# One pool of four PSUM banks for layer 1 of a fused attention and two feed-forward layers, with the attention of later batches merged into fewer TensorE visits and placed anew

## Chip, core and metric

One core of a Trainium2 chip runs the whole program. The metric is the device time in microseconds (us) of one execution. TensorE, VectorE, ScalarE and GpSimd appear as PE, DVE, ACT and POOL; SyncE (SP) issues the DMAs.

## What is computed

Attention with 32 landmarks (a Nystrom approximation), then two feed-forward layers on its 2304 x 512 output. B, H, S, D are 4, 8, 576, 64, and m is 32:

```python
q_lm = q.reshape(B, H, m, S // m, D).mean(axis=3)
k_lm = k.reshape(B, H, m, S // m, D).mean(axis=3)
A, Bm, C = sm(q, k_lm), sm(q_lm, k_lm), sm(q_lm, k)     # sm: scaled scores, softmax
Z = Bm^T / (norm1(Bm) * norminf(Bm) + 1e-6)
for _ in range(6):
    Z = 2 * Z - Z @ Bm @ Z
x = A @ Z @ C @ v                                       # heads back into rows of 512
h = x @ w_in;  x = (h * clip(h + 3, 0, 6) / 6) @ w_out                      # layer 1
h = x @ w2_in; out = (P(h) / (Q(h) + 1e-6)) @ w2_out                        # layer 2
```

Inputs are drawn as float64 for the weights (the kernel reads their bits as 64-bit integers and makes float32 of them) and the output is float32.

## The kernel before, in words

The work runs in two stages. **Layer 1** holds the attention of the four batches and the first feed-forward layer; **layer 2** is a pipeline of its own at the end of `fused` and is not touched by the diff.

Layer 1 works on blocks of 288 tokens (two a batch, eight in all) and on 16 chunks of 128 hidden features per block, 128 chunks in all. For each chunk `l1_in` multiplies U by A: six matmuls of 128x288 in float32r into a bank `psh`. U = T x w_in is the product of the attention's small matrix T (per head, 64x32) with the first weight, so that A x U is the hidden layer. ScalarE then makes the relu `r` and VectorE the gate `g` (the clipped product), which frees the bank. `l1_split` splits g into a high and a low half, `ghl` (ScalarE and GpSimd), and `l1_out` multiplies it by the second weight: twelve matmuls into four banks `psy`, which add up over the 16 chunks of a block. `l1_out` of a chunk stands LEAD = 3 chunks behind its `l1_in`.

Between the chunks stand the attention of the next batch and the conversion of weights (`cv_bits`: one operation on ScalarE and three on VectorE per slab of 128x1024; `cv_split` and stores behind it). The attention of a batch from 1 on is a chain: landmarks; the scores of C and of the landmark matrix (`scores_c`); transposes of exp(C) (`transpose_e`); `landmark_matrix`; the first E and V of the Newton iteration (`first_e`, `first_v`); six steps `newton` for each of two groups of four heads, which hold E as a 128x128 matrix with four 32x32 blocks on the diagonal and V beside it; T (`tmat`); the softmax of A for each half of the tokens (`scores_a`, `soft_a1` to `soft_a3`); and four `u_pair`, each of which makes U of one pair of slabs out of two slabs `wis` loaded again from DRAM. `by_head` issues the matmuls for eight heads: 64 rows by 32 columns each, four heads into either of two banks.

PSUM has eight banks: four `psy`, two `psa` for the attention, two `psh` for chunks (in batch 0 also for attention).

What sets the order: every piece of work is put into a list `plan` with a place, counted in chunks (`at`), and the list is emitted sorted by place. Numbers in `PRM` give the places of the start and of the conversions; for batches 1 to 3 `chain_c`, `chain_a` and the loop over `b` give them as fixed offsets. A scheduler in the framework then moves instructions on each engine's queue, so that the queues do not follow the plan exactly. All DMAs go through SP's queue in order. Slabs of weights, U and parts of y share 31 buffers.

Of the kernel before, what the change touches and what calls it, by code (L numbers as in the profile page):

```python
# [20 lines left out]
LM = 32  # L21
# [30 lines left out]
    d2=0,
    ta=5.46,
# [7 lines left out]
def fused(ctx: ExitStack, tc: tile.TileContext, qT, kT, v, w_in, w_out, w2_in, w2_out, ca, cb, out):  # L61
# [131 lines left out]
    def psa(tag="psa"):  # L193
        return pp.tile([P, 512], F32, tag=tag, name=tag, bufs=2 if tag in ("psa", "psh") else 1)
# [37 lines left out]
    def scores_a(b, h):  # L232
        sT = att.tile([P, 18, LM], F32, tag="sT", name="sT", bufs=1)
        pss = [psa("psh" if b == 0 else "psa") for _ in range(2)]
        by_head(
            pss, slice(0, HB),
            lambda r, a: kx[b][r:r + 64, a, S:S + LM],
            lambda r, a: qx[b][r:r + 64, a, h * HB:(h + 1) * HB],
        )
        for g in range(2):  # L240
            V.transpose(sT[:, 9 * g:9 * g + 9, :].rearrange("p a m -> p (a m)"), pss[g][:, :HB])
        st[b, h, "sT"] = sT
# [27 lines left out]
    def scores_c(b):  # L270
# [3 lines left out]
        end = [psa() for _ in range(2)]  # L274
        by_head(
            end, slice(0, TN + LM),
            lambda r, a: qs[r:r + 64, a, :], lambda r, a: kx[b][r:r + 64, a, 512:S + LM],
        )
        if b == 0:
            far = end  # L280
            big = [psa("psh") for _ in range(2)]
        else:

            far = []
            for g in range(2):
                t = att.tile([P, TN + LM], F32, tag=f"ce{g}", name="ce", bufs=1)
                A.activation(t, end[g][:, 0:TN + LM], AF.Copy)
                far.append(t)
            big = [psa() for _ in range(2)]
# [15 lines left out]
        for g in range(2):  # L305
            e = att.tile([P, S], F32, tag="e", name="e", bufs=2)
# [7 lines left out]

    def landmark_matrix(b):
# [4 lines left out]
        V.tensor_tensor(sm[:, :, 2], sm[:, :, 0], sm[:, :, 1], op=ALU.add)  # L320
# [29 lines left out]
        st[b, "bd"], st[b, "rc"] = bd, rc  # L350
# [13 lines left out]
    def first_e(b, g):  # L364
        bd, rc = st[b, "bd"], st[b, "rc"][:, 1]
        ps = psa()
        t = bd[:, 1, g].rearrange("p a m -> p (a m)")
        PE.matmul(ps[:, 0:P], t, t, start=True, stop=True)
        ev = att.tile([P, P + D], F32, tag=f"ev{g}", name="ev", bufs=2)
# [3 lines left out]
    def first_v(b, g):
        eT, rc, ev = st.pop((b, g, "eT")), st[b, "rc"][:, 0], st[b, g, "ev"]
        ps = psa("psh" if b == 0 else "psa")
        for c in range(5):
            n = P if c < 4 else 64
            for h in range(4):
                PE.matmul(
                    ps[LM * h:LM * h + LM, 0:D],  # L380
                    eT[0:n, c, LM * h:LM * h + LM],
                    vx[b][0:n, c, (2 * h + g) * D:(2 * h + g + 1) * D],
                    start=(c == 0), stop=(c == 4),
                )
        A.activation(ev[:, P:P + D], ps[:, 0:D], AF.Copy, scale=rc[:, g:g + 1])

    def newton(b, g, k):
        ev = st[b, g, "ev"]
        nx = att.tile([P, P + D], F32, tag=f"ev{g}", name="ev", bufs=2)
        last = k == NITER - 1  # L390
        if b == 0:

            x = ev[:, P:P + D]
# [7 lines left out]
            PE.matmul(vs, ev[:, 0:P], x, start=True, stop=True)  # L401
            if not last:
                V.tensor_tensor(nx[:, P:P + D], vs, x, op=ALU.add)
            else:
                V.tensor_tensor(nx[:, 0:D], vs, x, op=ALU.add)
        else:
            n0 = P if last else 0
            ps = psa()
            vs, x = ps[:, P:P + D], ev[:, P:P + D]
            PE.matmul(ps[:, n0:P + D], ev[:, 0:P], ev[:, n0:P + D], start=True, stop=True)  # L410
            if not last:
                A.activation(nx[:, 0:P], ps[:, 0:P], AF.Copy)
# [428 lines left out]
```

## Time and profile before

| | us |
|---|---|
| median of 3 runs (lowest, highest) | 873.9 (870.58, 874.69) |
| the profiled execution | 875.29 |
| its span in the profile | 873.5 |
| PE busy | 834.2 (96%) |
| PE weight loads busy | 748.6 (86%) |
| DVE, ACT, POOL busy | 577.2 (66%), 474.9 (54%), 483.2 (55%) |

Busy is the time in which at least one instruction of the engine runs. Matmuls overlap in the record (a 128x288 matmul is recorded with some 300 ns but the next one starts 130 ns later), so the pace of starts tells more than the length of one. A float32 matmul stands twice in the trace and once in the order listings. The profile has the span, its shares by engine, groups of instructions by line, the waits, the chain of work that ended last, and stretches of time with the busy time of each engine.

### The profile page before, as it was taken

The page shows a single profiled execution, that of the slowest core. Times are in us where ns is not written, and L with a number is a line of the kernel's source. Part 1 is how long each engine was busy: PE and PEld are TensorE (multiplying, and loading weights), DVE is VectorE, ACT ScalarE, POOL GpSimd, SP SyncE. Part 2 cuts the span into 40 slices and gives each one's busy share as a digit, 9 for nine tenths or more (in the row PEclk, how much of TensorE's full clock was granted, in tenths as well). Part 3 has the DMA queues.
Part 4 walks back from the last instruction along what each step waited for, and adds up shares of the span by engine and source line. Part 5 has one row for each costly group of instructions (what it writes and reads, how often), then busy time and mean ns, then how long its engine had stood idle before and what let it go on. Part 6 is the DMA issues. An engine that isn't in the chain of part 4 may idle for free.

```text
span 873.5 us, 14948 instructions
## 1 busy us (share of the span) xinstructions
PE 834.2 (96%) x5766; PEld 748.6 (86%) x5766; DVE 577.2 (66%) x910; ACT 474.9 (54%) x876; POOL 483.2 (55%) x353
## 2 busy tenths in 40 slices
PE   9679989999999899998999999999999999999998
PEld 8558879788977789888999899898998998989986
DVE  6967895776576945766215876765766666666566
ACT  3434654465445634655434666565665655656564
POOL 1438364465345533577331886766676685675542
PEclk9768999999999999999999999999999999999999
DMA  9765464669148740595797010010010010000000
GB/s 354 275 226 168 147 229 167 225 201 334 38 158 287 253 163 28 189 327 197 262 324 254 1 37 8 30 37 1 37 37 1 37 36 1 37 1 1 37 1 36
DMA packets 46310, 113.16 MB, mean 130 GB/s; under 512 B 6176, under 2 KB 14368, under 8 KB 45856
## 3 DMA queue, kind: packets, MB, share of 16 engines
q1 hardware_dynamic: 46240, 112.22, 36.7%
q8 instruction: 45, 0.74, 0.3%
q14 instruction: 25, 0.20, 0.1%
HBM read 81.79 MB, written 30.41 MB: 128 GB/s over the span
## 4 chain that ended last, share of the span: by engine, by line
PE 66%; DVE 15%; DMA 6%; ACT 6%; issue 4%; POOL 2%; SPq 0%; DVEq 0%; ACTq 0%; POOLq 0%
PE po L740 20%; PE ph L687 20%; PE psy L490 14%; PE psh L467 7%; DMA raw<-in_moe_w_out 3%; DVE val L142 2%; DVE val L143 2%; PE psa L227 2%; DMA qx<-in_q 2%; DVE g L472 1%; ACT val L140 1%; PE psa L410 1%; DVE val L141 1%; DMA yr<-yd 1%; DMA yd<-y 1%
## 5 line engine op out<-in xcount | busy, mean ns | idle before, releaser
L490 PE MATMUL psy<-ghl,whi 128*128 128x288 f32 x1024 | 225.3, 304 | 6.7 <-POOL ghl L99 4.4
L99 POOL TENSOR_TENSOR ghl<-g,ghl 128x288 fp32r<-128x288 f32 x128 | 127.4, 999 | 151.8 <-ACT ghl L94 143.1
L740 PE MATMUL po<-w2s,g2hl 128*128 128x512 f32 x864 | 209.6, 396 | 1.5 <-POOL g2hl L99 1.5
L687 PE MATMUL ph<-yhl,w2s 128*128 128x384 f32 x1152 | 208.5, 336 | 0.6 <-DVE y L518 0.6
L687 PEld LDWEIGHTS ph<-yhl,w2s 128*128 128x128 f32 x1152 | 202.1, 188 | 4.5 <-DVE y L518 0.8
L740 PEld LDWEIGHTS po<-w2s,g2hl 128*128 128x128 f32 x864 | 161.3, 188 | 37.9 <-POOL g2hl L99 2.9
L490 PEld LDWEIGHTS psy<-ghl,whi 128*128 128x128 f32 x1024 | 169.7, 191 | 16.9 <-issue 7.3
L490 PE MATMUL psy<-ghl,wlo 128*128 128x288 f32 x512 | 150.4, 299 | 0.0
L467 PE MATMUL psh<-AT,us 128*128 128x288 f32 x768 | 134.7, 308 | 12.5 <-DVE g L472 11.4
L467 PEld LDWEIGHTS psh<-AT,us 128*128 128x128 f32 x768 | 112.9, 194 | 25.5 <-DVE g L472 16.3
L717 DVE SCALAR_TENSOR_TENSOR q<-q,r 128x768 f32<-128x768 f32 (+1 forms) x52 | 46.6, 896 | 114.2 <-ACT r L712 114.2
L699 POOL TENSOR_SCALAR q<-t,cb_s 128x768 f32<-128x768 f32 x44 | 56.5, 1283 | 100.9 <-ACT t L697 100.9
L99 POOL TENSOR_TENSOR g2hl<-g,g2hl 128x768 fp32r<-128x768 f32 (+1 forms) x52 | 89.7, 1726 | 32.4 <-ACT g2hl L94 32.4
L472 DVE SCALAR_TENSOR_TENSOR g<-r,psh 128x288 f32<-128x288 f32 x128 | 56.8, 448 | 73.4 <-ACT r L470 65.2
L94 ACT ACTIVATE ghl<-g 128x288 fp32r<-128x288 f32 x128 | 56.2, 442 | 83.1 <-DVE g L472 75.9
L490 PEld LDWEIGHTS psy<-ghl,wlo 128*128 128x128 f32 x512 | 97.8, 191 | 0.9 <-issue 0.9
L470 ACT ACTIVATE r<-psh,three 128x288 f32<-128x288 f32 x128 | 63.1, 498 | 56.8 <-PE psh L467 56.6
L711 ACT ACTIVATE r<-q,lnb 128x768 f32<-128x768 f32 (+1 forms) x52 | 46.2, 889 | 81.8 <-POOL q L700 76.3
L99 POOL TENSOR_TENSOR wlo<-val,whi 128x1024 fp32r<-128x1024 f32 x24 | 59.9, 2496 | 52.1 <-ACT whi L94 48.9
L700 POOL TENSOR_TENSOR q<-q,t 128x768 f32<-128x768 f32 x44 | 84.5, 1920 | 3.7
L697 ACT ACTIVATE t<-ph 128x384 f32<-128x384 f32 x96 | 46.9, 489 | 56.5 <-PE ph L687 55.9
L718 DVE SCALAR_TENSOR_TENSOR p<-p,ca_s,r 128x768 f32<-128x768 f32 (+1 forms) x52 | 64.6, 1243 | 0.0
(144 smaller groups left out, 1016.3 us busy)
## 6 DMA issues: line engine op xcount, KB each, us to landing
raw<-in_moe_w_in SPq DMA_DIRECT2D x32, 512.0 KB, 5.9
raw<-in_moe_w_out SPq DMA_DIRECT2D x32, 512.0 KB, 5.3
wis<-wid SPq DMA_DIRECT2D x24, 512.0 KB, 7.4
w2s<-w2di SPq DMA_DIRECT2D x16, 512.0 KB, 6.0
w2s<-w2do SPq DMA_DIRECT2D x16, 512.0 KB, 5.9
yd<-y SPq DMA_DIRECT2D x32, 144.0 KB, 2.9
out<-o SPq DMA_DIRECT2D x18, 256.0 KB, 2.0
vx<-in_v SPq DMA_DIRECT2D x4, 1024.0 KB, 8.5
```

Source lines behind the costliest of these rows:

```text
L94: A.activation(dst_hi, src, AF.Copy)
L99: lo_eng.tensor_tensor(dst_lo, src, dst_hi.bitcast(F32), op=ALU.subtract)
L467: PE.matmul(ps[:, :HB], u[:, wp, f0:f0 + P], at[:, xp, g, :], start=(k == 0), stop=(k == 5))
L470: A.activation(r, ps[:, :HB], AF.Relu, bias=three)
L472: V.scalar_tensor_tensor(gg, in0=r, scalar=6.0, in1=ps[:, :HB], op0=ALU.min, op1=ALU.mult)
L490: PE.matmul(ps[e][:, :HB], w1[c // 2][wp][:, o + e * P:o + (e + 1) * P], t[:, xp, :], start=(c == c0 and i == 0), stop=(c == c1 and i == 2),)
L687: PE.matmul(ps[i][:, :T2], w2i[u][wp][:, d * 256 + i * P:d * 256 + (i + 1) * P], yh[:, xp, d, :], start=(k == 0), stop=(k == 11),)
L697: A.activation(t[:, i], h, AF.Abs)
L699: eng.tensor_scalar(q[:, cs], t[:, cs], cb_s[:, 1:2], cb_s[:, 0:1], op0=ALU.mult, op1=ALU.add)
L700: eng.tensor_tensor(q[:, cs], q[:, cs], t[:, cs], op=ALU.mult)
L718: V.scalar_tensor_tensor(p, in0=p, scalar=ca_s[:, 0:1], in1=r, op0=ALU.add, op1=ALU.mult)
L740: PE.matmul(ops[j][m], t[:, xp, i, m * P:(m + 1) * P], w2o[u][wp][:, i * DM:(i + 1) * DM], start=(c == 0 and k == 0), stop=(c == NFC - 1 a ...
```

## The change

- `psa` gives banks `psa` and `psh` one tag `psx` with four buffers; `l1_in` takes its bank from there. LEAD becomes 4 and `ghl` has five buffers in place of four.
- For batches 1 to 3 `scores_ca` makes the scores of A's first half, of C and of the landmark matrix in one visit of four banks, and copies C to SBUF unscaled; `soft_c` makes the maxima and exponentials from there. `scores_a` still makes A's second half.
- For batches 1 to 3 Newton's E is kept twice: the 128x128 block-diagonal matrix and its 32 columns without the zeros. A step multiplies 96 columns (32 of E, 64 of V) in place of 192, and VectorE spreads the 32 columns over the diagonal again with the mask `m4`. `first_e` makes both forms, with a new constant `id4`.
- `u_visit` makes U of two slab pairs (four slabs `wis`) in one visit of four banks; in batch 0 still one pair a visit.
- The places of batches 1 to 3 are three rows of 44 numbers (`bt`), one for each piece of work, held in a legal order by `placed`. The places of the start, of batch 0 and of the conversions also move.

The diff, cut to its core:

```diff
-    return pp.tile([P, 512], F32, tag=tag, name=tag, bufs=2 if tag in ("psa", "psh") else 1)
+    return pp.tile([P, 512], F32, tag="psx" if tag in ("psa", "psh") else tag, name=tag, bufs=4 if tag in ("psa", "psh") else 1)
...
+    def scores_ca(b):
+
+        qs = st.pop((b, "qs"))
+        one, two = [psa() for _ in range(2)], [psa() for _ in range(2)]
+        a_heads(b, 0, one)
+        by_head(
+            one, slice(HB, HB + TN + LM),
+            lambda r, a: qs[r:r + 64, a, :], lambda r, a: kx[b][r:r + 64, a, 512:S + LM],
+        )
+        by_head(
+            two, slice(0, 512),
+            lambda r, a: qs[r:r + 64, a, :], lambda r, a: kx[b][r:r + 64, a, 0:512],
+        )
+        sT = att.tile([P, 18, LM], F32, tag="sT", name="sT", bufs=1)
+        for g in range(2):
+            e = att.tile([P, S + LM], F32, tag="e", name="e", bufs=2)
+            A.activation(e[:, 512:S + LM], one[g][:, HB:HB + TN + LM], AF.Copy)
+            V.transpose(sT[:, 9 * g:9 * g + 9, :].rearrange("p a m -> p (a m)"), one[g][:, :HB])
+            A.activation(e[:, 0:512], two[g], AF.Copy)
+            st[b, g, "e"] = e
+        st[b, 0, "sT"] = sT
+
+    def soft_c(b):
+        mx = att.tile([P, 2, 2], F32, tag="cmx", name="cmx", bufs=2)
+        for g in range(2):
+            e = st[b, g, "e"]
+            V.tensor_reduce(mx[:, g, 0:1], e[:, 0:S], axis=AX.X, op=ALU.max)
+            V.tensor_reduce(mx[:, g, 1:2], e[:, S:S + LM], axis=AX.X, op=ALU.max)
...
         else:
-            n0 = P if last else 0
+            n0 = LM if last else 0
             ps = psa()
-            vs, x = ps[:, P:P + D], ev[:, P:P + D]
-            PE.matmul(ps[:, n0:P + D], ev[:, 0:P], ev[:, n0:P + D], start=True, stop=True)
+            PE.matmul(ps[:, n0:LM + D], ev[:, 0:P], ev[:, P + n0:v0 + D], start=True, stop=True)
             if not last:
-                A.activation(nx[:, 0:P], ps[:, 0:P], AF.Copy)
-                V.tensor_tensor(nx[:, P:P + D], vs, x, op=ALU.add)
-            else:
-                V.tensor_tensor(nx[:, 0:D], vs, x, op=ALU.add)
+                V.tensor_tensor(
+                    nx[:, 0:P].rearrange("p (a m) -> p a m", m=LM), ps[:, 0:LM].unsqueeze(1).to_broadcast([P, 4, LM]), m4,
+                    op=ALU.mult,
+                )
+                if k < NITER - 2:
+                    A.activation(nx[:, P:v0], ps[:, 0:LM], AF.Copy)
+            V.tensor_tensor(nx[:, v0:v0 + D], ps[:, LM:LM + D], x, op=ALU.add)
...
-    def u_pair(b, u):
+    def u_visit(b, us):
 
         T = st[b, "T"]
-        pss = [psa() for _ in range(2)]
-        for s in range(2):
...
+        pss = {u: [psa() for _ in range(2)] for u in us}
+        for u in us:
+            for s in range(2):
+                w = wi.pop((b, 2 * u + s))
...
-            (2, lambda: scores_c(b)),
-            (4, lambda: transpose_e(b, 0)),
...
+            (scores_ca, b), (soft_c, b), (transpose_e, b, 0), (landmark_matrix, b), (transpose_e, b, 1),
+            (first_e, b, 0), (first_e, b, 1), (first_v, b, (0, 1)),
+        ] + [(newton, b, g, k) for k in range(NITER) for g in range(2)] + [
+            (tmat, b), (soft_a1, b, 0), (soft_a2, b, 0), (soft_a3, b, 0),
+            (scores_a, b, 1), (soft_a1, b, 1), (soft_a2, b, 1), (soft_a3, b, 1),
+        ] + [(wi_load, b, j) for j in range(NG)] + [(u_visit, b, (0, 1)), (u_visit, b, (2, 3))]
...
-    LEAD = 3
+    LEAD = 4
```

On TensorE's queue the U products of batch 1 (`psa<-wis,T`) stood before in pieces of 8 and 16 between chunks (`psh`, `psy`):

```order
L227 MATMUL psa<-wis,T 32x256 x8
L467 MATMUL psh<-AT,us 128x288 x6
L227 MATMUL psa<-wis,T 32x256 x8
L467 MATMUL psh<-AT,us 128x288 x2
L490 MATMUL psy<-ghl,whi 128x288
L490 MATMUL psy<-ghl,wlo 128x288
L490 MATMUL psy<-ghl,whi 128x288 x2
L490 MATMUL psy<-ghl,wlo 128x288
L490 MATMUL psy<-ghl,whi 128x288 x2
L490 MATMUL psy<-ghl,wlo 128x288
L227 MATMUL psa<-wis,T 32x256 x16
```

Now, at the first U visit of the same batch:

```order
L520 MATMUL psh<-AT,us 128x288 x6
L543 MATMUL psy<-ghl,whi 128x288
L543 MATMUL psy<-ghl,wlo 128x288
L543 MATMUL psy<-ghl,whi 128x288
L543 MATMUL psy<-ghl,wlo 128x288
L232 MATMUL psa<-wis,T 32x256 x32
L543 MATMUL psy<-ghl,whi 128x288 x2
L543 MATMUL psy<-ghl,wlo 128x288
```

Four slabs now stand together, with four psy matmuls between the last chunk's psh and the visit.

The Newton steps on TensorE's queue (`psa<-ev`) stood before, in batch 2, one group at a time:

```order
L467 MATMUL psh<-AT,us 128x288 x6
L410 MATMUL psa<-ev 128x192
L490 MATMUL psy<-ghl,whi 128x288 x2
L490 MATMUL psy<-ghl,wlo 128x288
L490 MATMUL psy<-ghl,whi 128x288
L410 MATMUL psa<-ev 128x192
```

Now, in batch 1, both groups of a step stand together:

```order
L458 MATMUL psa<-ev 128x96 x2
L520 MATMUL psh<-AT,us 128x288 x6
L458 MATMUL psa<-ev 128x96 x2
L520 MATMUL psh<-AT,us 128x288 x6
L232 MATMUL psa<-val,T 32x256 x16
L458 MATMUL psa<-ev 128x96 x2
```

In all the first layer's queue has 17 pieces of `psa<-wis,T` before and 9 now.

On VectorE's queue the maxima of C's scores in batch 1 (`cmx`) stood before between gates of chunks (`g<-r,psh`):

```order
L295 TENSOR_REDUCE cmx<-ce 128x1
L296 TENSOR_REDUCE cmx<-ce 128x1
L295 TENSOR_REDUCE cmx<-ce 128x1
L296 TENSOR_REDUCE cmx<-ce 128x1
L472 SCALAR_TENSOR_TENSOR g<-r,psh 128x288
L302 TENSOR_SCALAR cnb<-cmx 128x2
L472 SCALAR_TENSOR_TENSOR g<-r,psh 128x288 x3
L298 TENSOR_REDUCE cmx<-psa 128x1 x2
L299 TENSOR_TENSOR cmx<-cmx 128x2
L472 SCALAR_TENSOR_TENSOR g<-r,psh 128x288
```

Now, after the tenth gate, the softmax of A's first half (`sT`, `mx`, `sm`) stands among them, ahead of the next gate:

```order
L330 STREAM_TRANSPOSE sT<-psa 128x288
L340 TENSOR_REDUCE cmx<-e 128x1
L330 STREAM_TRANSPOSE sT<-psa 128x288
L340 TENSOR_REDUCE cmx<-e 128x1
L255 TENSOR_REDUCE mx<-sT 128x18
L343 TENSOR_SCALAR cnb<-cmx 128x2
L256 TENSOR_TENSOR sT<-sT,mx 128x576
L339 TENSOR_REDUCE cmx<-e 128x1 x2
L262 TENSOR_REDUCE sm<-sT 128x18
L342 TENSOR_SCALAR cnb<-cmx 128x2
L525 SCALAR_TENSOR_TENSOR g<-r,psh 128x288
```

Before, those pieces of A stood behind the 22nd gate.

## Rows read from the trace of the kernel before

**Rows 1.** Stretches of the run: from:to, length, busy time of each engine, clock, DMA.

```profile
core 0: us, PE busy (x) PEld busy (x) DVE busy (x) ACT busy (x) POOL busy (x), PEclk, DMA share, GB/s
70.40:464.50 394.10, 375.98 (x3287) 340.68 (x3286) 246.51 (x437) 202.87 (x439) 198.48 (x165) 0.99 0.60 207
67.30:129.70 62.40, 58.33 (x534) 52.80 (x535) 53.08 (x87) 36.65 (x80) 37.71 (x28) 0.97 0.54 178
92.60:125.90 33.30, 29.51 (x320) 25.68 (x319) 31.54 (x49) 22.00 (x46) 18.79 (x13) 1.00 0.56 179
175.10:279.80 104.70, 100.62 (x941) 88.47 (x939) 70.72 (x131) 54.81 (x123) 53.20 (x46) 1.00 0.59 203
279.80:383.30 103.50, 97.70 (x877) 88.17 (x875) 65.84 (x121) 54.50 (x120) 46.94 (x40) 0.98 0.53 185
383.30:464.50 81.20, 77.14 (x554) 75.05 (x552) 29.72 (x45) 36.81 (x75) 43.36 (x39) 0.98 0.78 272
407.00:457.00 50.00, 50.00 (x379) 50.00 (x378) 13.11 (x26) 22.07 (x48) 21.13 (x24) 1.00 0.79 276
464.50:873.50 409.00, 403.29 (x2016) 362.76 (x2016) 275.33 (x371) 243.33 (x381) 257.78 (x160) 1.00 0.08 28
```

**Rows 2.** TensorE, 70.4 to 464.5 us: L490 as stretch, then groups.

```profile
70.40:464.50 394.10, 242.91 (x1536) 216.45 (x1536) 0.99 0.60 207
L467 PE MATMUL psh<-AT,us 128*128 128x288 f32 x745 | 128.6, 304 | 7.5 <-DVE g L472 7.2
L227 PE MATMUL psa<-wis,T 64*32 64x256 f32 x384 | 18.4, 383 | 1.1 <-DMA wis<-wid 1.0
```

**Rows 3.** Timeline of TensorE around a U product: start, length, instructions.

```profile
160.79 0.29 PE L490 MATMUL psy<-ghl,whi 128*128 128x288 f32 x1
161.02 1.09 PE L227 MATMUL psa<-wis,T 64*32 64x256 f32 x32
162.04 0.40 PE L490 MATMUL psy<-ghl,whi 128*128 128x288 f32 x1
162.28 0.30 PE L490 MATMUL psy<-ghl,wlo 128*128 128x288 f32 x1
```

**Rows 4.** The same, around one bank's part of a U product.

```profile
167.15 1.07 PE L227 MATMUL psa<-wis,T 64*32 64x256 f32 x16
168.15 0.54 PE L467 MATMUL psh<-AT,us 128*128 128x288 f32 x2
```

**Rows 5.** The same, around the scores of A for one bank.

```profile
154.85 0.69 PE L227 MATMUL psa<-qx,kx 64*32 64x288 f32 x8
155.47 0.40 PE L490 MATMUL psy<-ghl,whi 128*128 128x288 f32 x1
```

**Rows 6.** The same, around one Newton step.

```profile
130.16 0.49 PE L410 MATMUL psa<-ev 128*128 128x192 f32 x2
130.35 0.43 PE L490 MATMUL psy<-ghl,whi 128*128 128x288 f32 x1
130.62 0.30 PE L490 MATMUL psy<-ghl,wlo 128*128 128x288 f32 x1
```

**Rows 7.** VectorE's groups, 67.3 to 130 us, then 70.4 to 464.5 us.

```profile
L142 DVE SCALAR_TENSOR_TENSOR val<-raw,val 128x1024 uint32<-128x1024 uint32 x8 | 11.3, 1418 | 0.1
L472 DVE SCALAR_TENSOR_TENSOR g<-r,psh 128x288 f32<-128x288 f32 x22 | 9.6, 443 | 4.1 <-ACT r L470 4.0
...
L413 DVE TENSOR_TENSOR ev<-psa,ev 128x64 f32<-128x64 f32 x30 | 6.5, 218 | 9.0 <-ACT ev L412 8.8
L247 DVE TENSOR_REDUCE mx<-sT 128x18 f32<-128x576 f32 x6 | 4.5, 753 | 0.2
L370 DVE SCALAR_TENSOR_TENSOR ev<-psa,rc,ident 128x128 f32<-128x128 f32 x6 | 2.0, 340 | 0.6 <-PE psa L368 0.6
```

**Rows 8.** ScalarE's copy of E in a Newton step.

```profile
L412 ACT ACTIVATE ev<-psa 128x128 f32<-128x128 f32 x30 | 8.2, 277 | 8.2 <-PE psa L410 8.0
```

**Rows 9.** TensorE's longest wait there: total us, times, longest.

```profile
PE psh L467 <- DVE g L472: 7.2, 9, 2.1
```

More of the change, by code (lines that the diff above doesn't have):

```diff
@@ L230, in fused, with a_heads @@
     SC2 = SC1 / SEG
-    def scores_a(b, h):
-        sT = att.tile([P, 18, LM], F32, tag="sT", name="sT", bufs=1)
-        pss = [psa("psh" if b == 0 else "psa") for _ in range(2)]
+    def a_heads(b, h, outs):
         by_head(
-            pss, slice(0, HB),
+            outs, slice(0, HB),
             lambda r, a: kx[b][r:r + 64, a, S:S + LM],
@@ L239, in scores_a @@
         )
+    def scores_a(b, h):
+        pss = [psa() for _ in range(2)]
+        a_heads(b, h, pss)
+        sT = att.tile([P, 18, LM], F32, tag="sT", name="sT", bufs=1)
         for g in range(2):
@@ L273, in scores_c @@
         mx = att.tile([P, 2, 4], F32, tag="cmx", name="cmx", bufs=2)
-        end = [psa() for _ in range(2)]
+        far = [psa() for _ in range(2)]
         by_head(
-            end, slice(0, TN + LM),
+            far, slice(0, TN + LM),
             lambda r, a: qs[r:r + 64, a, :], lambda r, a: kx[b][r:r + 64, a, 512:S + LM],
         )
-        if b == 0:
-            far = end
-            big = [psa("psh") for _ in range(2)]
-        else:
[L284 to L289, printed above, removed]
+        big = [psa() for _ in range(2)]
         by_head(
@@ L367, in first_e, with first_v @@
         t = bd[:, 1, g].rearrange("p a m -> p (a m)")
+        if b > 0:
+            PE.matmul(ps[:, P:P + LM], t, st[b, "bm"][:, 1, g], start=True, stop=True)
         PE.matmul(ps[:, 0:P], t, t, start=True, stop=True)
[L369 removed]
+        ev = att.tile([P, P + LM + D], F32, tag=f"ev{g}", name="ev", bufs=2)
         V.scalar_tensor_tensor(ev[:, 0:P], in0=ps[:, 0:P], scalar=rc[:, g:g + 1], in1=ident, op0=ALU.mult, op1=ALU.add)
+        if b > 0:
+            V.scalar_tensor_tensor(
+                ev[:, P:P + LM], in0=ps[:, P:P + LM], scalar=rc[:, g:g + 1], in1=id4, op0=ALU.mult, op1=ALU.add
+            )
         st[b, g, "ev"] = ev
[L373 to L385, printed above, removed]
+    def first_v(b, gs):
+        rc = st[b, "rc"][:, 0]
+        ps = psa()
+        for g in gs:
+            eT = st.pop((b, g, "eT"))
+            for c in range(5):
+                n = P if c < 4 else 64
+                for h in range(4):
+                    PE.matmul(
+                        ps[LM * h:LM * h + LM, g * D:(g + 1) * D],
+                        eT[0:n, c, LM * h:LM * h + LM],
+                        vx[b][0:n, c, (2 * h + g) * D:(2 * h + g + 1) * D],
+                        start=(c == 0), stop=(c == 4),
+                    )
+        for g in gs:
+            ev = st[b, g, "ev"]
+            A.activation(ev[:, P + LM:P + LM + D], ps[:, g * D:(g + 1) * D], AF.Copy, scale=rc[:, g:g + 1])
     def newton(b, g, k):
         ev = st[b, g, "ev"]
[L389 removed]
+        nx = att.tile([P, P + LM + D], F32, tag=f"ev{g}", name="ev", bufs=2)
         last = k == NITER - 1
+        v0 = P + LM
+        x = ev[:, v0:v0 + D]
         if b == 0:
[L393 removed]
             if not last:
@@ L461, in l1_in @@
         f0 = (c % 4) * P
[L462 removed]
+        ps = psa("psh")
         k = 0
@@ L582, in at, with placed @@
         plan.append((place, len(plan), f, a))
+    def placed(places, needs):
+        out = []
+        for t, i in zip(places, needs):
+            out.append(max([t] + [out[j] + 1e-4 for j in i]))
+        return out
     def warm(n, x):
```

155 lines of the change are left out of this document (73 added, 82 removed), and 3 rows, old and new, of the table bt.

## The prediction, made before the result was known

> **What bounds the kernel now.** I read the stretches first, then the groups on TensorE inside layer 1, then single visits on the timeline, and last who makes TensorE wait. The stretches [rows 1] cut the run in two. From 464.5 us to the end, 409.0 us, the second layer keeps TensorE busy for 403.3 us; the diff touches nothing there, so I carry these 409 us over unchanged. What can move is the first layer, 70.4 to 464.5 us: 394.1 us, in which TensorE is busy 376.0 us and idle 18.1 us, at a granted clock of 0.99, so the clock is not what holds it. Where only the feed-forward runs (407 to 457 us) 379 matmuls fill 50 us, that is 0.132 us each, and a chunk of 18 of them takes 2.4 us. The 1536 + 745 matmuls of this kind in the stretch [rows 2] would fill 301 us at that pace. The other 93 us are the attention of batches 1 to 3 on TensorE ("visits") and waiting. So the questions are what a visit costs, how many go away, and whether another engine then takes over.
>
> **What a visit costs.** A U product of one slab pair, its 32 matmuls alternating between two banks, runs from 161.02 to 162.04 us: 1.02 us [rows 3]. Around it the spacing of the main matmuls is 0.23 and 0.24 us in place of 0.13, so entering and leaving costs another 0.2 us. Where the scheduler has put only one bank's 16 matmuls in a row, they take 1.00 us [rows 4]: half the work in the same time. The scores of A for one bank, 8 matmuls, take 0.62 us [rows 5], and by the comparison of rows 3 and 4 both banks' 16, alternating, should take the same 0.62. One Newton step of one group takes 0.19 us and makes the next interval 0.27 in place of 0.13: 0.33 in all [rows 6].
>
> **U of four slabs a visit.** Before: 18.4 us busy [rows 2] in 17 pieces of TensorE's order, so 18.4 + 17 x 0.2 = 21.8 us. After: 12 slab pairs at 1.02 and 9 pieces at 0.2 give 14.0. Some of the 18.4 was waiting, not work, so I take 7 us off.
>
> **Scores in one visit.** Before, each batch has four one-bank visits of 0.62 and two of C, each with its 0.2; after, two visits with 0.62 for each half of A and C's time unchanged. That saves 2 x 0.62 + 4 x 0.2 = 2.0 us a batch, 6 us.
>
> **Newton without zeros.** Ten single steps of 192 columns (0.33 each) become five pairs of two times 96 columns, the same columns as one single, so about 0.33 a pair; the last pair saves a switch. 1.8 us a batch, and 5 us in all after one pair that the order splits. The small extra matmul of the first E (32 columns, six of them) costs 0.3 us in all at the pace of rows 6. Together TensorE loses **18 us** of work, 6 a batch.
>
> **What goes to VectorE.** E's copy was one ScalarE operation of 0.277 us [rows 8]; now VectorE multiplies it out of PSUM with the mask (I take 0.34 us, the row of the same size from PSUM; the low end is the 0.218 of the 64-column add; the high end is doubled by the access with a repeated operand, 0.7) [rows 7]. Ten a batch: 3.4 us (2 to 7). In batches 2 and 3 this lies beside TensorE's work: VectorE is busy 70.7 of 104.7 and 65.8 of 103.5 us there [rows 1], and 4 us more still leave 25. In batch 1 it does not. Between 67.3 and 129.7 us VectorE works off the conversions of weights and the 22 first gates [rows 7] and is busy 53.1 of 62.4 us, in the middle (92.6 to 125.9) 31.5 of 33.3. The new order puts the first half's softmax of A (transposes, two reductions, a subtraction of 0.75 us each and the like), the whole Newton chain and its adds of 0.22 us ahead of the 22nd gate, where most of it stood behind: counted from the order, 15 us more. 53 + 15 = 68 us, and 72 with the 5% idle of the middle: the 22nd gate comes 6 to 9 us later than before. After it, TensorE has less left than before, 12 chunks at 2.4 us and two U visits of 2.2 against the 45.4 us that it took from 129.7 to 175.1: some 35. So the first batch ends near 67.3 + 70 + 35 = 172 against 175.1. I take 2 us off there, not 6.
>
> Which engine counts in that stretch is the point to weigh. By its matmul rows TensorE is busy 29.5 of the 33.3 us and looks as full as VectorE.
>
> The Trainium skill, Perfetto Trace Analysis, Identifying the Most-Contended Engine, says to judge TensorE by weight loading, since matmul slices overlap, and VectorE by occupancy. Here that is 25.7 us against 31.5 us, so by that rule VectorE binds and whatever is put on it there is paid in full; matmul occupancy would have promised the full 6 us. By the rule the sum ends near 876, by matmul occupancy near 855.
>
> The trace agrees with the rule for the middle of the stretch (5% idle), less for the whole of it (9 of 62 us idle), and my 2 us stand between.
>
> **The wait that is added, and the one that goes.** Nine visits (three of scores, six of U) now need all four shared banks: the last two or three chunks must have been read by ScalarE and VectorE first. TensorE's queue is in order, so the psy matmuls behind such a visit wait with it. A chunk needs about 0.95 us after its last matmul to be read (the gate is 0.443 [rows 7]; the relu before it is of like size), and an operation of a conversion in front adds up to 1.4 us. Bounds: nothing to 2.4 us a visit; I take 0.7, since the order keeps psy matmuls of chunks already split in front of most of them: 6 us. Against this, four banks and a lead of four chunks in place of two and three should remove most of the 7.2 us that psh now waits for the gate [rows 9]. These two I let cancel, and keep the idle time of 18 us. Loads: the slabs of U are requested in fours, so SP's queue holds more of them ahead of raw weights and y stores; DMA is busy 0.60 of the stretch [rows 1], and I put this at nothing with 3 us either way. Front (to 70.4 us): the same conversions and the same Newton for batch 0, nothing to 1 us either way. The end, 383.3 to 464.5: last conversions a little more spread, TensorE idle 4.1 us there; 1 us off.
>
> **Sum.** 2 + 6 + 6 + 1 = 15 us. The profiled execution took 875.3 us (span 873.5), so 860.3; it lies 1.4 us above the median of the runs, so **859 us**. Its own range, from 18 us saved plus 4 of idle time to 8 us saved: 852 to 866.
>
> **Rivals.**
> - *The waits go too.* Four banks in rotation and the longer lead free TensorE of most waits, not only of visits. For it: the largest single cause of TensorE's idle time is the gate that frees a psh bank [rows 9]. Against: the visits take the same banks. Ten of the 18 us idle go: 849.
> - *VectorE takes the first batch.* The stretch to 129.7 us grows by all 15 us, and TensorE's savings of that batch do nothing: + 15 - 6 - 6 - 1 = +2, 877, 876 at the median. For it: 31.5 of 33.3 us. Against: part of the moved work can run in the 9 us in which VectorE now idles, and the stretch after it gets lighter. This is what the Trainium skill's rule named above would make of it.
> - *Four banks at once block TensorE.* This ends slower. Each of the nine visits waits for its last bank, and the next chunks for four copies of about 0.6 us on ScalarE and as many subtractions on VectorE. The gain of 15 is gone at (15 + 6) / 9 = 2.3 us a visit; at 3.5 us the sum is 875.3 - 15 - 6 + 31.5 = 885.8, at the median 884. For it: in the first batch only 11 psy matmuls (1.5 us) stand behind the scores. Against: 47 of them stand behind those of batch 3, and 12 to 36 in most other places.
>
> **How the numbers follow.** The forecast has 0.58, the waits going too 0.14, VectorE 0.17, blocked banks 0.11. A measurement of this kernel can tell 0.5%, 4.4 us, from no change: below 869.5 is faster, above 878.3 slower. Faster: 0.57 of the forecast, 0.14 and 0.02 of VectorE's case: 0.73. Within: 0.01 and 0.13 of VectorE's, 0.01 of the blocked banks: 0.15. Slower: 0.12. The range for 8 in 10 takes in the forecast's own, nearly all of the faster case and half of VectorE's: 848 to 874.
>
> **What would show it.** In the new profile U should stand in pieces of about 2.0 us, scores of a batch in one piece near 2.0, and a Newton pair in 0.2 + 0.14; the first layer's stretch should be near 380 us; the 22nd gate of VectorE should end between 134 and 140 us; layer 2 should still take 409 us. If a merged visit of A costs twice 0.62, if VectorE's mask product takes 0.7 us, if psh or the score visits stand under TensorE's waits with more than 10 us, or if VectorE's 22nd gate comes after 145 us, the step named is wrong.

## The result and the profile after

The changed kernel takes **851.8 us** (median of 4 runs, 849.4 to 854.9) against 874.3: ratio 0.975, interval 0.971 to 0.980. The profiled execution takes 851.85 with a span of 850.1, so 23.4 us of span are gone. First the stretches of the changed kernel, as in [rows 1] (from:to, length, busy time of PE, PEld, DVE, ACT and POOL, clock, DMA); the second row is the first batch's stretch up to the psy of the 32nd chunk, the third the part of it between the 8th and the 16th:

```profile
65.80:440.10 374.30, 361.17 (x3299) 337.23 (x3298) 248.77 (x461) 201.64 (x427) 208.09 (x167) 0.99 0.64 222
65.80:171.80 106.00, 101.01 (x981) 91.44 (x980) 90.07 (x160) 60.72 (x128) 64.20 (x49) 0.99 0.61 209
90.70:123.80 33.10, 29.40 (x320) 25.59 (x319) 30.09 (x61) 20.32 (x45) 19.41 (x13) 1.00 0.62 204
171.80:267.00 95.20, 93.80 (x895) 87.47 (x894) 70.38 (x136) 55.28 (x116) 55.58 (x44) 1.00 0.67 234
267.00:366.00 99.00, 93.93 (x888) 86.37 (x886) 61.65 (x124) 51.31 (x115) 48.67 (x41) 0.98 0.49 168
366.00:440.10 74.10, 72.43 (x540) 71.95 (x540) 26.68 (x43) 34.32 (x70) 39.63 (x36) 1.00 0.83 297
440.10:850.10 410.00, 404.17 (x2016) 363.21 (x2016) 275.35 (x371) 243.42 (x381) 257.37 (x160) 1.00 0.08 28
```

| stretch (first psy of chunk) | before | after | difference |
|---|---|---|---|
| start to the first psy | 70.4 | 65.8 | -4.6 |
| batch 1 (chunks 0 to 32) | 104.7 | 106.0 | +1.3 |
| batch 2 (32 to 64) | 104.7 | 95.2 | -9.5 |
| batch 3 (64 to 96) | 103.5 | 99.0 | -4.5 |
| end of layer 1 (96 to 128) | 81.2 | 74.1 | -7.1 |
| layer 2 | 409.0 | 410.0 | +1.0 |

The same 23.4 us by kind: in layer 1 TensorE is busy 361.2 us in place of 376.0 [rows 1], 14.8 less; idle 374.3 - 361.2 = 13.1 in place of 18.1, 5.0 less; it starts 4.6 earlier; layer 2 takes 1.0 more. The rows count TensorE's work at whatever clock it had. The psh matmuls of a stretch shift a little, since some are done ahead. Their rows (weight loads in the second bracket), first the kernel before, batch 1 and end, then the changed one:

```profile
70.40:175.10 104.70, 33.25 (x193) 27.32 (x192) 0.99 0.53 185
383.30:464.50 81.20, 27.24 (x170) 23.91 (x168) 0.98 0.78 272
```

```profile
65.80:171.80 106.00, 34.22 (x205) 29.70 (x204) 0.99 0.61 209
366.00:440.10 74.10, 25.01 (x156) 22.22 (x156) 1.00 0.83 297
```

Batch 1 now holds 204 in place of 192; at 0.133 us these 12 are 1.6 us, so without them it stands at 104.4: unchanged. The end holds 156 in place of 168, which is 1.6 of its 7.1.

What stands in TensorE's rows now, a visit of four slabs, the score visit of batch 1, a Newton pair (timeline: start, length, instructions):

```profile
155.42 1.96 PE L232 MATMUL psa<-wis,T 64*32 64x256 f32 x64
157.30 0.54 PE L543 MATMUL psy<-ghl,whi 128*128 128x288 f32 x2
```

```profile
81.54 0.71 PE L232 MATMUL psa<-qx,kx 64*32 64x288 f32 x16
82.05 2.37 PE L232 MATMUL psa<-kx,qs 64*32 64x96 f32 x32
84.34 0.53 PE L543 MATMUL psy<-ghl,whi 128*128 128x288 f32 x2
```

```profile
201.76 0.58 PE L458 MATMUL psa<-ev 128*128 128x96 f32 x4
202.13 0.65 PE L520 MATMUL psh<-AT,us 128*128 128x288 f32 x3
```

Four slabs take 1.9 us, from start to the next start, where [rows 3] needed 1.02 for two. A Newton pair takes 0.36; the interval behind it is 0.22 in place of 0.13 in the trace, so it costs 0.45 in all, where two single steps as in [rows 6] cost 0.65. The merged score visit takes 2.80 us, from 81.54 to 84.34, and not the 2.0 that I named: the second row, C with its 96- and 512-column matmuls, holds 2.3 of it. It stands in one piece in batch 1 only: the order splits it into three pieces in batch 2 and two in batch 3. The groups, and who makes TensorE wait in layer 1 (total us, times, longest):

```profile
L520 PE MATMUL psh<-AT,us 128*128 128x288 f32 x745 | 121.4, 301 | 1.9 <-DVE us L496 1.0 <-DVE g L525 0.9
L232 PE MATMUL psa<-wis,T 64*32 64x256 f32 x384 | 13.3, 381 | 0.8 <-DMA wis<-wid 0.5 <-DVE g L525 0.3
```

```profile
PE psy L543 <- POOL ghl L104: 5.2, 5, 2.1
PE psy L543 <- ACT y L569: 2.2, 1, 2.2
PE psy L543 <- DVE y L571: 1.6, 1, 1.6
PE psh L520 <- DVE g L525: 0.9, 1, 0.9
PE psa L232 <- DVE g L525: 0.3, 1, 0.3
```

U went from 18.4 us in 17 pieces [rows 2] to 13.3 in 9. The wait of psh for the gate, 7.2 us [rows 9], is down to 0.9, and the four-bank visits themselves wait for almost nothing (U for the gate: 0.3). The waits of psy are most of what is left.

### The profile page after: what moved, and what is told of

It is laid out like the page before. It is cut to its first block, busy times and chain, and to the rows that moved or that the text cites. A ratio compares the mean times of both kernels' runs of the same rounds, so it can differ in the third digit from the quotient of the medians.

```text
span 850.1 us, 14978 instructions
## 1 busy us (share of the span) xinstructions
PE 818.7 (96%) x5778; PEld 743.3 (87%) x5778; DVE 576.8 (68%) x935; ACT 473.4 (56%) x864; POOL 486.9 (57%) x353
## 4 chain that ended last, share of the span: by engine, by line
PE 61%; DVE 15%; DMA 9%; ACT 5%; POOL 4%; issue 4%; SPq 0%; DVEq 0%; ACTq 0%; POOLq 0%
PE po L783 21%; PE ph L730 20%; PE psy L543 12%; PE psh L520 5%; DMA raw<-in_moe_w_in 3%; DMA qx<-in_q 3%; DVE val L148 3%; DVE val L147 2%; DMA yd<-y 2%; PE psa L232 1%; ACT val L145 1%; DVE val L146 1%; DVE g L525 1%; POOL ghl L104 1%; DMA wis<-wid 1%
## 5 line engine op out<-in xcount | busy, mean ns | idle before, releaser
L543 PE MATMUL psy<-ghl,whi 128*128 128x288 f32 x1024 | 217.8, 300 | 9.6 <-POOL ghl L104 5.2
L104 POOL TENSOR_TENSOR ghl<-g,ghl 128x288 fp32r<-128x288 f32 x128 | 135.0, 1064 | 120.2 <-ACT ghl L99 113.2
L543 PEld LDWEIGHTS psy<-ghl,whi 128*128 128x128 f32 x1024 | 167.7, 190 | 20.2 <-POOL ghl L104 6.7
L520 PE MATMUL psh<-AT,us 128*128 128x288 f32 x768 | 127.8, 305 | 7.0 <-ACT us L495 3.4
```

The lines of the kernel that those rows point to most:

```text
L104: lo_eng.tensor_tensor(dst_lo, src, dst_hi.bitcast(F32), op=ALU.subtract)
L520: PE.matmul(ps[:, :HB], u[:, wp, f0:f0 + P], at[:, xp, g, :], start=(k == 0), stop=(k == 5))
L543: PE.matmul(ps[e][:, :HB], w1[c // 2][wp][:, o + e * P:o + (e + 1) * P], t[:, xp, :], start=(c == c0 and i == 0), stop=(c == c1 and i == 2),)
```

## Experiments

The theory I set out with, of **visits**: layer 1 is as long as TensorE's own work in it, and each break in the row of main matmuls costs 0.23 us (the main matmuls of layer 1 exceed their pace of 0.133 us by 22.8 us in 97 pieces before and 13.9 in 58 after, counted from start to start with idle time left out: 8.9 / 39). That figure is at its upper end, since matmuls at a lower clock count as excess too: with the lead alone, in a run below, the excess falls to 20.0 us though the pieces rise to 100. Around single visits the two longer intervals add 0.2 us [rows 3]. Its rivals: the **buffers** (pool and lead) did it, or the **places** did. Ratios are to the kernel before on the same chip. The changed kernel's own interval is 3.6 us to either side, so differences to it of some 4 us are just at the edge of what can be told; two runs below that change it little give 851.8 and 852.0 with 2 us to either side.

### Is it the buffers? The kernel before with pool and lead, and with the lead alone

```diff
-    return pp.tile([P, 512], F32, tag=tag, name=tag, bufs=2 if tag in ("psa", "psh") else 1)
+    return pp.tile([P, 512], F32, tag="psx" if tag in ("psa", "psh") else tag, name=tag, bufs=4 if tag in ("psa", "psh") else 1)
-    LEAD = 3
+    LEAD = 4
-    t = w1p.tile([P, 2, HB], F32R, tag="ghl", name="ghl", bufs=4)
+    t = w1p.tile([P, 2, HB], F32R, tag="ghl", name="ghl", bufs=5)
```

> The kernel before with one pool of four banks and LEAD 4 (five ghl buffers) alone, before at 874.3. By the theory of visits (the first layer's length is TensorE's own work there: attention work plus 0.23 us for each piece of it that breaks the row of main matmuls) only the 7 us of psh waits and some ten pieces go: 863 to 867, with about 90 pieces of main matmuls and psh waits under 2 us. By the theory of waits (the buffers did it) most of the 22 us comes: 853 to 859.

Measured: 862.9 us, ratio 0.986 (0.984 to 0.988): half of the gain without a single merged visit, at the lower edge of what the theory of visits allowed and well short of the other. In the trace 87 pieces of main matmuls are left of 97.

```profile
PE psa L227 <- DVE g L472: 5.6, 3, 2.1
PE psy L490 <- POOL ghl L99: 2.1, 3, 1.3
```

The wait of psh for the gate has gone from the list, but three U visits (one of batch 0's U, two of later ones) now wait for the same gate, 5.6 us in all: with the old places the shared pool moves the wait rather than removes it. The second run has only the lines on LEAD and `ghl`:

> The kernel before with LEAD 4 and five ghl buffers alone (banks still two and two). If the lead is what took 11 us off in the run with pool and lead, 863 to 866 with the last stretch (from the 96th chunk's psy to the end of layer 1, 81.1 before, 74.9 there) near 75. If it is the pool, 872 to 875. By the theory of visits the pool makes the visits (17 pieces of scores and 14 of U in place of 20 and 17), so the lead's part is the last stretch alone: 867 to 870.

Measured: **865.5 us**, ratio 0.989 (0.988 to 0.991). The lead alone gives 9.8 us, more than the theory of visits had for it. The fifth buffer is in that too; a run below keeps it at LEAD 3. The pool adds 1 to 3 us by these medians, which is no more than the intervals of the two runs. Its waits and its stretches (all of layer 1, and from the psy of the 96th chunk):

```profile
PE psh L467 <- DVE g L472: 6.5, 7, 1.8
PE psy L490 <- POOL ghl L99: 2.0, 5, 0.7
```

```profile
70.40:454.70 384.30, 372.63 (x3287) 337.99 (x3286) 241.32 (x436) 202.65 (x439) 199.10 (x165) 1.00 0.62 213
378.40:454.70 76.30, 74.20 (x548) 72.69 (x546) 28.20 (x41) 33.87 (x70) 39.94 (x35) 1.00 0.79 280
```

The psh wait is nearly what it was (6.5 for 7.2); what went is the other kind. In the kernel before, TensorE also waited for these, of which the second has gone whole:

```profile
PE psy L490 <- POOL ghl L99: 4.4, 4, 2.1
PE psy L490 <- ACT y L516: 1.5, 1, 1.5
```

and the longest of them did more than its 2.07 us. The timeline and the clock there:

```profile
396.71 0.69 PE L490 MATMUL psy<-ghl,whi 128*128 128x288 f32 x4
399.47 0.61 PE L490 MATMUL psy<-ghl,whi 128*128 128x288 f32 x1 [2.07 <-POOL ghl L99]
399.88 0.44 PE L490 MATMUL psy<-ghl,wlo 128*128 128x288 f32 x1
400.12 0.44 PE L490 MATMUL psy<-ghl,whi 128*128 128x288 f32 x1
```

```profile
394.00:406.00 12.00, 9.81 (x61) 9.34 (x60) 7.70 (x9) 6.89 (x11) 9.41 (x6) 0.86 0.64 221
```

Behind the wait the matmuls start 0.24 us apart in place of 0.13: the granted clock of these 12 us is 0.86, part of it at the lower level of 1.2 GHz, where it is 1.00 from 407 us on [rows 1]. With LEAD 4 the stretch from the 96th chunk takes 76.3 us against 81.2, at 1.00. All told TensorE's idle time falls from 18.1 to 384.3 - 372.6 = 11.7 us and its busy time by 3.4, with three pieces more. Of the 6.4 us of idle time 2.4 are this wait for ghl, 1.5 the wait for y and 1.7 a wait of the first E; the rest are small ones.

### The lead taken out of the changed kernel, with and without its buffer, and lengthened

```diff
-    LEAD = 4
+    LEAD = 3
-    t = w1p.tile([P, 2, HB], F32R, tag="ghl", name="ghl", bufs=5)
+    t = w1p.tile([P, 2, HB], F32R, tag="ghl", name="ghl", bufs=4)
```

> The changed kernel with LEAD 3 and four ghl buffers. By the theory of visits the pieces stay as they are (60 and 60 in the order), so only waits for ghl and the last stretch come back: 855 to 858, last stretch 76 to 80 in place of 74.0. If the lead matters nothing beside merged visits: 851 to 853. If the four-bank visits need the longer lead (a chunk split must be ready to fill TensorE's queue in front of them): 860 or more, psx waits in the visits of U and of the scores over 8 us.

Measured: 861.1 us, ratio 0.984 (0.982 to 0.985), 9.2 us slower than the changed kernel. The time is that of the third case, the reason is not: the visits wait little, psy waits for ghl.

```profile
PE psy L543 <- POOL ghl L104: 6.9, 6, 3.4
PE psy L543 <- ACT ghl L99: 3.0, 1, 3.0
PE psa L232 <- DVE g L525: 1.4, 1, 1.4
```

```profile
65.50:448.80 383.30, 363.51 (x3299) 338.28 (x3298) 247.73 (x463) 201.69 (x428) 204.34 (x167) 0.99 0.62 216
87.40:128.10 40.70, 31.25 (x316) 27.18 (x315) 35.23 (x68) 22.03 (x46) 19.18 (x13) 0.92 0.63 216
98.00:118.00 20.00, 12.27 (x133) 10.25 (x136) 19.09 (x33) 7.21 (x12) 7.47 (x5) 0.84 0.63 217
```

The stretches are all of layer 1, the part between the 8th and the 16th chunk's psy, and 20 us in it. In those 20 us VectorE is busy 19.1 and TensorE 12.3, at a granted clock of 0.84; the part takes 40.7 us against 33.1. The last stretch stayed at 74.4: most of the loss is in batch 1 (112.6 us against 106.0), not where I expected it. Now LEAD 3 with the fifth buffer kept:

```diff
-    LEAD = 4
+    LEAD = 3
```

> The changed kernel with LEAD 3 and five ghl buffers. LEAD 3 with four gave 861.1. If the distance counts, the fifth buffer changes nothing: 859 to 862. If the buffer counts, 851 to 854.

Measured: 860.4 us, ratio 0.985 (0.983 to 0.987). The distance counts; the buffer by itself does nothing here. One more, with five buffers:

```diff
-    LEAD = 4
+    LEAD = 5
```

> The changed kernel with LEAD 5 and still five ghl buffers. LEAD 3 cost 9 us here and gave TensorE 6 us more idle time, mostly waits of psy for ghl. If the distance between a chunk's gate and its psy matmuls is what counts, one more gives 1 to 3 us: 848.5 to 851. If with LEAD 4 those waits have already gone to other causes (y copies, U), 851 to 853; if five buffers are then too few, over 856 with psh or ghl waits.

Measured: 866.4 us, ratio 0.991 (0.989 to 0.994): 14.6 us slower. More distance isn't simply better. They are lost in batch 1 (116.5 us against 106.0) and batch 2 (103.2 against 95.2), at a granted clock of 0.93 and 0.97 in place of 0.99 and 1.00. The largest wait of TensorE is neither psh's nor ghl's: it stands 5.4 us before the first E of batch 1 (wait, and the stretches of the two batches):

```profile
PE psa L409 <- DVE bm L377: 5.4, 1, 5.4
```

```profile
65.70:182.20 116.50, 106.80 (x986) 95.53 (x985) 91.97 (x160) 62.62 (x131) 62.93 (x50) 0.93 0.56 191
182.20:285.40 103.20, 99.07 (x899) 90.82 (x895) 72.85 (x136) 55.24 (x117) 56.26 (x45) 0.97 0.63 219
```

That one wait is a third of the loss. Five buffers may also be too few at this distance: ScalarE's part of the split waits for the psy matmuls that free a ghl buffer twice as long in layer 1 as in the changed kernel. First the changed kernel, then this run:

```profile
ACT ghl L99 <- PE psy L543: 6.6, 5, 2.8
```

```profile
ACT ghl L99 <- PE psy L543: 12.6, 13, 2.2
```

No run has a sixth buffer, and the places stayed those made for LEAD 4, so what makes LEAD 5 slow is open.

### One part undone at a time

U of one pair a visit, the second pair 1.5 chunks behind the first:

```diff
-        ] + [(wi_load, b, j) for j in range(NG)] + [(u_visit, b, (0, 1)), (u_visit, b, (2, 3))]
+        ] + [(wi_load, b, j) for j in range(NG)] + [(u_visit, b, (0,)), (u_visit, b, (1,)), (u_visit, b, (2,)), (u_visit, b, (3,))]
...
```

> The changed kernel with U of one slab pair a visit in batches 1 to 3. By the theory of visits ten more pieces at 0.23 us: 2.3 us more, 853 to 855, the U matmuls themselves still about 13 us. If four-bank visits cost TensorE waits that two-bank ones do not, it is no slower, 849 to 852.

Measured: 856.2 us, ratio 0.979 (0.978 to 0.981), 16 pieces of U in the trace, 4.4 us more where ten breaks would be 2.3, as the matmuls themselves take longer too (13.3 in the changed kernel). The group, and layer 1:

```profile
L232 PE MATMUL psa<-wis,T 64*32 64x256 f32 x384 | 16.9, 383 | 0.0
```

```profile
65.40:444.10 378.70, 369.03 (x3299) 338.06 (x3298) 249.56 (x461) 200.66 (x427) 206.15 (x167) 0.99 0.62 219
```

TensorE's idle time is 378.7 - 369.0 = 9.7 us here against 13.1, its busy time 7.9 us longer. So four banks at once may cost waits elsewhere, in the psy matmuls around them, though less than they save; one trace of each doesn't settle it.

The Newton step as before:

```diff
...
-            PE.matmul(ps[:, n0:LM + D], ev[:, 0:P], ev[:, P + n0:v0 + D], start=True, stop=True)
+            PE.matmul(ps[:, n0:P + D], ev[:, 0:P], ev[:, n0:P + D], start=True, stop=True)
...
-                V.tensor_tensor(
-                    nx[:, 0:P].rearrange("p (a m) -> p a m", m=LM), ps[:, 0:LM].unsqueeze(1).to_broadcast([P, 4, LM]), m4,
-                    op=ALU.mult,
-                )
+                A.activation(nx[:, 0:P], ps[:, 0:P], AF.Copy)
```

> The changed kernel with the Newton step of before (192 columns, E copied by ScalarE, no mask product on VectorE) at the new places. By the theory of visits 96 more columns a step and some six pieces more: 3 to 5 us, 855 to 857. If VectorE is what counts in the first batch, losing the mask product there gives back: the first batch's stretch (106.0 us from the first psy to the 32nd chunk's) gets 2 us shorter and the whole comes to 851 to 853.

Measured: 856.7 us, ratio 0.980 (0.978 to 0.981). The first batch's stretch is 106.4 against 106.0: taking the mask products off VectorE (busy 87.6 us there in place of 90.1) didn't shorten it. TensorE has more to do in it, though (102.9 us in place of 101.0), so this run alone doesn't settle who sets the stretch. The scores in three visits of two banks:

```diff
-            (scores_ca, b), (soft_c, b), (transpose_e, b, 0), (landmark_matrix, b), (transpose_e, b, 1),
+            (scores_c1, b), (soft_c, b), (transpose_e, b, 0), (landmark_matrix, b), (transpose_e, b, 1),
...
+            if f is scores_c1:
+                at((b - 1) * 32 + t + 0.8, scores_c2, b)
+            elif f is soft_c:
+                at((b - 1) * 32 + t + 0.8, scores_a, b, 0)
```

> The changed kernel with the merged visit of scores taken apart into three of two banks (the end of C with the landmark matrix, the 512 columns of C, A's first half), copies as in the changed kernel. By the theory of visits two visits more a batch at 0.23 us and 0.3 to 0.6 us of matmuls that no longer overlap: 3 to 5 us, 855 to 857. If the four-bank visit costs in waits what it saves: 850 to 853.

Measured: 860.4 us, ratio 0.985 (0.983 to 0.987), 8.5 us slower, more than the visits account for: there are 61 pieces in place of 58. Most of it is in batch 1 (113.4 us against 106.0). Between the 8th and 16th chunk, and the worst 20 us of it:

```profile
88.60:131.10 42.50, 37.34 (x339) 30.59 (x340) 35.37 (x72) 22.20 (x46) 17.96 (x12) 0.84 0.63 215
101.40:121.40 20.00, 17.90 (x169) 13.77 (x169) 15.65 (x29) 8.66 (x15) 7.08 (x5) 0.66 0.57 196
```

For 20 us the granted clock is 0.66 on average, so (1 - 0.66) x 2, two thirds, of that time at the lower level, and the part takes 42.5 us against 33.1 at 1.00. `soft_c` stands about 1.1 chunks later here, so the delay of the chain counts with the visits; this run can't part them. The places of batches 1 to 3 back at fixed offsets:

```diff
-        for t, (f, *a) in zip(placed(PRM["bt"][b - 1], needs), later(b)):
+        for t, (f, *a) in zip(placed(row, needs), later(b)):
```

> The changed kernel with the places of batches 1 to 3 put back to the fixed offsets of before (a U visit at the mean of the places of its two pairs). By the theory of visits the pieces are 67 in place of 60, 1.6 us, and some waits come back: 853 to 858. By the theory that the places did it (each step moved to where an engine is free) 862 or more, and the gain over before under 12 us.

Measured: 862.7 us, ratio 0.986 (0.984 to 0.988): 10.8 us slower than the changed kernel, with 65 pieces of main matmuls in the trace against 58. The theory of places has it here. Its layer 1:

```profile
66.90:452.70 385.80, 369.20 (x3299) 340.08 (x3298) 254.42 (x461) 200.61 (x427) 202.28 (x167) 0.99 0.62 215
```

Against the changed kernel TensorE is busy 369.2 - 361.2 = 8.0 us more and idle 16.6 - 13.1 = 3.5 us more.

### The start, and VectorE in batch 1

The places of the start put back (`f`, `a0`, `a1`, `u0` and the first eight of `cv`):

```diff
-    u0=-5.4,
+    u0=-4.88,
...
-    f=[-78.2, -63.24, -60.85, -62.05, -59.74, -59.16, -58.38, -57.2, -56.3, -55.43, -55.23, -53.49, -53.31, -53.27, -52.82, -50.61, -43.53, -46.73, -41.98],
+    f=[-78.2, -66.29, -60.85, -60.84, -59.74, -59.16, -58.38, -57.2, -56.3, -55.43, -55.23, -53.48, -53.3, -53.26, -53.12, -50.6, -49.07, -46.73, -35.19],
```

> The changed kernel with the places of the start (batch 0's chain, its softmax of A, the first eight conversions, the first U) as before. If those places brought the start of the first psy from 70.4 to 65.8 us: 69 to 71 us here, and 855 to 857 in all. If it came from the shared pool, 65 to 67 and 851 to 853.

Measured: 851.8 us, ratio 0.973 (0.971 to 0.975); first psy at 66.9. Those places brought at most 1.1 of the 4.6 us, and nothing in the whole. Then the places inside a conversion alone:

```diff
-            at(cvp[i] + 0.1 * h, cv_bits, convs[i], h)
+            at(cvp[i] + 0.4 * h, cv_bits, convs[i], h)
...
-    fin=1.11,
+    fin=1.82,
```

> The changed kernel with the conversion's inner places as before (its two halves 0.4 apart in place of 0.1, its split 1.82 behind in place of 1.11). The old places of the start alone left the first psy at 66.9 us, so if these steps brought the 4.6 us of the start, the first psy is at 69 to 71 us and the whole at 855 to 857; if neither did, and the shared code of the start did it, 65 to 67 us and 851 to 853.

Measured: 856.1 us, ratio 0.980 (0.978 to 0.982); first psy at 71.5. The halves of a conversion and its split standing closer together are what brings the start forward; which of the two steps does it, this run can't tell. One row of VectorE's timeline shows most of it, the copy of batch 0's T that ends its Newton chain: before, changed, and this run.

```profile
53.67 0.29 DVE L428 COPY T<-psa 128x128 f32<-128x128 f32 x1
```

```profile
48.06 0.28 DVE L479 COPY T<-psa 128x128 f32<-128x128 f32 x1
```

```profile
51.51 0.25 DVE L479 COPY T<-psa 128x128 f32<-128x128 f32 x1
```

It came 5.6 us earlier, and with the old inner places 3.4 of them are lost again.

Last, the softmax of A without its shift by the maximum:

```diff
-        V.tensor_reduce(mx, sT, axis=AX.X, op=ALU.max)
-        (G if b == 0 else V).tensor_tensor(sT, sT, mx.unsqueeze(2).to_broadcast([P, 18, LM]), op=ALU.subtract)
```

(for batches 1 to 3 only).

> The changed kernel without the maximum and its subtraction in the softmax of A of batches 1 to 3 (the shift that cancels in the quotient is left out): two VectorE operations of 0.75 us for each half less, 3.0 us a batch. If VectorE sets the first batch's stretch (106.0 us), it gets 1.5 to 3 us shorter and those of batches 2 and 3 (95.1 and 99.1) by under 1: 848 to 850.5. If TensorE sets all three: all within 1 us of those, 851 to 853.

Measured: 852.0 us, ratio 0.974 (0.972 to 0.976). The first batch's stretch:

```profile
66.40:173.60 107.20, 101.68 (x981) 91.45 (x980) 86.90 (x157) 61.52 (x129) 64.58 (x49) 0.99 0.60 208
```

VectorE has 90.07 - 86.9 = 3.2 us less to do in the stretch, and it takes 107.2 us in place of 106.0. So 3 us of VectorE's work less do not shorten it; its queue's order changed a little with it, so the order is not excluded. No version tried is clearly faster than the changed kernel.

The theory that is left: the gain has four parts, TensorE's shorter and fewer visits; the longer lead, which keeps psy from waiting (and the granted clock of batch 1 at 0.99, where LEAD 3 has 0.96); a start that is earlier by the order inside conversions; and places for batches 1 to 3 without which, in batch 1 above all, half of the gain is given back (10.8 of 22.5 us). That each part counts is shown; how much each gives by itself is not.

## Why the prediction was right, and where its steps were off

The median of 851.8 lies in the range of 848 to 874, on the side that was given 0.73. It lies 7 us under the forecast of 859 and, by a hair, under the forecast's own range of 852 to 866. That it lies in the range owes much to the range's width: 22.5 us were gained and 15 summed, and the start and the end, both priced near nothing, make up more than the difference. The three batches were to give 14 us and gave 12.7, but with the shares turned round. The terms, in the order of the sum:

- **Work on TensorE: 18 us forecast, 14.8 measured**, and the kind of saving as described, but the 14.8 are not all visits: the lead by itself took 3.4 us off TensorE's busy time in the kernel before, and without it the changed kernel has 2.3 more, so the visits' own part is nearer 12 (an estimate from these two). U's visits take 1.9 us where 2.04 was taken, and U as a whole gives the 7 us named: 18.4 - 13.3 and eight breaks at 0.23. The scores were over-rated: added from start to next start they went from 12.4 to 10.3 us, with 11 pieces fewer at 0.23 that is 4.6 and not 6, and the 2.0 us that I named for a merged visit left out most of C, 2.3 us by itself. Newton was over-rated too: a pair costs 0.45 with the longer interval behind it, where 0.33 was forecast, so it saves 0.2 us and not 0.33, some 3 us for fifteen pairs and not 5.
- **6 us a batch: no.** Batch 1 gave nothing, batch 2 9.5, batch 3 4.5. That the first batch pays back was right in kind: VectorE's 22nd gate ended at 135.6 us (134 to 140 forecast), 72.5 us after the first one in place of 62.4. That is 10.1 us more where 6 to 9 were forecast; the time itself was met because the start came 4.6 us earlier, which was not forecast.

```profile
135.19 0.44 DVE L525 SCALAR_TENSOR_TENSOR g<-r,psh 128x288 f32<-128x288 f32 x1
```

  But the reason given, VectorE's sum of work, fell with the run that takes 3 us of it away and gains nothing. The Trainium skill, Perfetto Trace Analysis, Identifying the Most-Contended Engine, takes the engine with the highest occupancy as the most contended one, which is VectorE in the middle of that stretch (30.1 of 33.1 us, against 25.6 of weight loading). That what is put on it there is paid in full, as the prediction drew from the rule, was not borne out: neither 3 us less nor the missing mask products (with 1.9 us more of TensorE's work there) shortened the stretch. Where the order is disturbed (LEAD 3), the 20 us with VectorE busy 19.1 do look as the rule says. What sets the stretch in the changed kernel, a chain over several engines or the order on VectorE's queue, stays open.
- **The mask product:** 0.34 us taken, 0.289 measured.

```profile
L460 DVE TENSOR_TENSOR ev<-psa,m 128x128 f32<-128x128 f32 x30 | 7.9, 289 | 13.0 <-PE psa L458 13.0
```

- **The step that failed: "These two I let cancel, and keep the idle time of 18 us."** Idle time fell by 5.0 us. The visits with four banks wait almost nothing themselves (0.3 us in all for U), not 0.7 each; and the lead, which I sized by the psh wait alone, acts on others. In the kernel before, 6.4 us of idle time go with it, of which the waits of psy for ghl and y are 3.9 and the psh wait 0.7, and 3.4 us of busy time, part of it matmuls at the lower clock; in the changed one the waits for ghl cost 5.2 us with it and 9.9 without. So "the clock is not what holds it" was too quick: 0.99 over the whole stretch hid 0.86 in the 12 us around one wait. The lead alone is worth 9.8 us in the kernel before and 9.2 in the changed one. The rows for it (4.4 and 1.5 us of waits, 0.86 in 12 us) were in the trace, and I priced only the first cause on the list.
- **"Front ... nothing to 1 us either way":** 4.6 us, and by the conversion's inner places. I counted the conversions of the start as the same work and did not look at how their operations stand between those of batch 0's chain on VectorE's queue.
- **The end: 1 us forecast, 7.1 measured**; 1.6 of it are psh matmuls done earlier, and with the lead alone the stretch was already 4.9 shorter. But with LEAD 3 the changed kernel has 74.4 there too, so the lead isn't needed for it, and what else shortens it stays open.
- **Layer 2: unchanged forecast, 1.0 us longer.** No run was made for it. Counted from its first matmul to the end it takes 408.5 us in all three runs of the kernel before, with pool or lead too, and 409.4 to 409.8 in every run of the changed one; so neither pool nor lead lengthens it, and the cause is open.

Among the rivals, "the waits go too" (849, given 0.14) is nearest to the time, but half its 10 us of idle time went, and the lead did more than the four banks. "Four banks at once block TensorE" is not seen at the visits: U waits 0.3 us for the gate.

The parts do not add up: undone one at a time they cost 4.4, 4.9, 8.5, 10.8, 9.2 and 4.2 us, 42 in all, for a gain of 22. Every one of the large ones lengthens batch 1 (111 to 113 us against 106), where places, lead and visits were laid for each other; and with LEAD 3 and with split scores the granted clock falls there (0.84 and 0.66 in 20 us). So what is lost when one part is undone is no measure of its share.

## What to carry to other kernels

Price every wait of the engine that sets the end, not only the largest, and look at the granted clock behind it: behind one wait of 2.07 us the matmuls ran at about half the pace for two more. Here a longer distance between producer and consumer, one chunk, was worth 9 to 10 us in either kernel. Changes laid out together (order, lead, visits) cannot be priced by undoing them one at a time: the losses here come to twice the gain. And an engine that is 90 to 95% busy in a stretch isn't by that alone its limit: take work off it and see whether the stretch moves.

## What the runs showed that I had not expected

A wait of 2.07 us was followed by matmuls 0.24 us apart for two more microseconds (granted clock 0.86 in the 12 us around it), and in the run with split scores a stretch of 20 us stood at 0.66. Another surprise is how much one step of the lead does either way: 3, 4 and 5 give 860, 852 and 866 us with the same places and five ghl buffers.
